# Spreading attention's reciprocal denominators over partitions: VectorE's stream shuffle in place of a 0/1 matrix product

## The chip, the cores and the metric

The kernel runs on one core of a Trainium2 chip. A core has TensorE (PE in the profile; its weight loads are listed as PEld), VectorE (DVE), ScalarE (ACT), GpSimd (POOL) and SyncE (SP), which here issues every DMA. They run side by side and wait for each other by semaphores; each one takes its own instructions in the order in which the program holds them. The metric is the device time of one execution in microseconds, the median of several runs.

## What is computed

Linear attention with an exponential feature map, followed by a gated feed-forward layer with a convolution over the sequence. Cut to what matters:

```python
batch, n_heads, seq, head_dim = (8, 8, 576, 64)      # d_feat = 128

def phi(x):
    proj = np.einsum('bhsd,df->bhsf', x, w_phi)
    proj = proj - np.max(np.abs(proj), axis=-1, keepdims=True)
    return np.concatenate([np.exp(proj), np.exp(-proj)], axis=-1)
q_p, k_p = (phi(q), phi(k))
kv = np.einsum('bhsf,bhsd->bhfd', k_p, v)
z = np.sum(k_p, axis=2)
num = np.einsum('bhsf,bhfd->bhsd', q_p, kv)
den = np.einsum('bhsf,bhf->bhs', q_p, z)[..., None] + 1e-06
attn = num / den                      # heads side by side: x of (8, 576, 512)

h = np.maximum(x @ w_in, 0.0)         # 512 -> 1024
conv_out = ...                        # 3 taps along the sequence, per column
gate = 1.0 / (1.0 + np.exp(-conv_out))
out = (h * gate) @ w_out              # 1024 -> 512
```

The place of the change is the division: `num` has a row of 576 values for each of 64 dimensions of a head, `den` has one such row per head.

## The kernel before

All matrix products are made of parts: a float32 operand is split into `hi`, its value in PE's float32r type, and `lo`, the rest, and three products (`hi·hi`, `hi·lo`, `lo·hi`) are summed in PSUM. The helper `split` (L57 to L65) does this with a copy and a subtraction on engines that the caller names.

**Layout.** Everything is transposed: features or channels lie over the 128 partitions, the sequence along the columns. A batch `b` has eight heads, in two quads `qd`; a quad has two pairs `pr`, and a pair `p = 2 qd + pr` puts two heads of 64 dimensions on the 128 partitions. The 576 positions come in five groups `g` for the attention, and in two halves `c` of 288 for the feed-forward layer (290 columns with the neighbours that the convolution needs, `HW`).

**Attention.** `k_process` loads and splits k and v, projects (`kp`, L203 to L205), takes the maximum and subtracts it on DVE (`km`, `ks`, L208 and L210), exponentiates on ACT and sums `kv` on PE (L255, L259). `q_process` does the same for q (`qp`, `qm`, `qs`), transposes on PE (`tp`, L324), exponentiates (L330), splits (`qh`, `ql`), and multiplies by `kv` (`nm`, L352 and L360). A column of ones in v makes the denominator the 65th row of `nm`. ACT copies the numerators into `num` (L383) and the denominator row into `dr` (L378), and a DMA reshapes that row into the tile `den` of 72 x 16 (L381), so that few columns have to be inverted.

**The division, `x_process` (L388 to L417).** For each batch and pair, 32 in all: DVE adds 1e-6 and inverts `den` (L396, L397); the reciprocals `rc` are split into two float32r parts (L399); four DMAs (L402) lay them out as rows 0 to 3 of the tile `rr` (two parts of two heads), a tile that exists once and is otherwise zero. Then for each half `c`: a product of `sel_r`, a 0/1 matrix made from the input `selr` at the start (L81 to L85), with 290 columns of `rr` writes into `rb` (L410): each partition gets the sum of the two parts of its head. DVE multiplies `num` by `rb` into `xf` (L412), and `xf` is split into `xh` (ACT) and `xl` (DVE), the inputs of the feed-forward layer.

**Feed-forward.** For each of 16 halves `n`: `hp` (L435, 96 products of 128x290), ReLU into `h` on ACT (L442), the convolution on POOL and DVE into `c` (L458, L463), a sigmoid (L467), a product (L471) and a split (`gh`, `gl`), and `op` (L494, 96 products of 128x288), copied out by ACT (L499) and stored (L500). The weights come in 64-bit form and are converted and split at the start (`weight_process`, L100 to L109), in large part on DVE.

**PSUM.** Three pools: `pg` with four buffers, shared by `kp`, `qp`, `tp`, `nm` and `rb`; `pm` with two, for `hp` and `op`; `pk` for the running `kv`.

**What sets the order.** A loop at the end (L564 on) runs generators as small processes, by an estimated clock `now` with PE costs (`yield pe(...)`) and delays (`yield wait(...)`), attention interleaved with feed-forward. This gives the order in which instructions are traced, with priorities: `x_process` runs under `tc.high_priority()`. A scheduler that lays the instructions on a timeline of its own then decides each engine's final order. So a change in one instruction moves others on all engines.

Of the kernel before, what the change touches and what calls it, by code (L numbers as in the profile page):

```python
# [7 lines left out]
F32 = mybir.dt.float32  # L8
F32R = mybir.dt.float32r
# [3 lines left out]
ALU = mybir.AluOpType  # L13
AX = mybir.AxisListType.X

B, H, S, D = 8, 8, 576, 64
F = 128
DM, FF = 512, 1024
P = 128
NQ = 2  # L20
TC = 288
HW = TC + 2
# [13 lines left out]
def kernel(  # L36
# [13 lines left out]
    nc = tc.nc  # L50
    cp = ctx.enter_context(tc.tile_pool(name="cp", bufs=1))
    sb = ctx.enter_context(tc.tile_pool(name="sb", bufs=1))
    pg = ctx.enter_context(tc.tile_pool(name="pg", bufs=4, space=bass.MemoryType.PSUM))
# [3 lines left out]
    def split(src, hi, lo, eng_hi, eng_lo):  # L57

        if eng_hi is nc.scalar:
            nc.scalar.activation(out=hi, in_=src, func=AF.Copy)  # L60
        elif eng_hi is nc.gpsimd:
            nc.gpsimd.tensor_scalar(out=hi, in0=src, scalar1=1.0, scalar2=0.0, op0=ALU.mult, op1=ALU.add)  # L62
        else:
            nc.vector.tensor_copy(out=hi, in_=src)
        eng_lo.tensor_tensor(out=lo, in0=src, in1=hi.bitcast(F32), op=ALU.subtract)  # L65
# [12 lines left out]
    split(wbd_f, wbd_hi, wbd_lo, nc.vector, nc.vector)  # L78
    idn = load_const(ident, [P, P], "idn")

    selr_f = sb.tile([P, P], F32, name="selr_f", tag="qr", bufs=2)  # L81
    nc.gpsimd.memset(selr_f, 0.0)
    nc.sync.dma_start(out=selr_f[:4, :], in_=selr)
    sel_r = cp.tile([P, P], F32R, name="sel_r")
    nc.gpsimd.tensor_copy(out=sel_r, in_=selr_f)  # L85
    rr = cp.tile([P, S], F32R, name="rr")
    nc.gpsimd.memset(rr.bitcast(F32), 0.0)

# [66 lines left out]
    def pe(ns):  # L157
        return ("pe", ns)
# [4 lines left out]
    def until(*keys):  # L163
        return ("until", [k for k in keys if k is not None])

    def set_ready(key, ns=0):
        ready[key] = now[0] + ns * LAT
# [136 lines left out]
    def q_process(b, qd, g):  # L304
# [80 lines left out]
        if g == 2 or g == 4:  # L385
            spawn(x_process(b, qd * 2 + g // 2 - 1))

    def x_process(b, p):  # L388
        yield ("wait", 4000)
        qd, pr = divmod(p, 2)  # L390
        dn, nt = den[b, qd, pr], numt[b, qd, pr]
        if 4 * b + p > 0:
            yield until(("x", *divmod(4 * b + p - 1, 4), 1))
        with tc.high_priority():
            rc = sb.tile([72, 16], F32, name=f"rc{b}_{p}", tag="rc", bufs=2)
            nc.vector.tensor_scalar(out=dn, in0=dn, scalar1=1e-6, scalar2=None, op0=ALU.add)  # L396
            nc.vector.reciprocal(out=rc, in_=dn)  # L397
            rhl = [sb.tile([72, 16], F32R, name=f"rc{j}{b}_{p}", tag=f"rc{j}", bufs=2) for j in range(2)]
            split(rc, rhl[0], rhl[1], nc.vector, nc.vector)  # L399
            for j in range(2):  # L400
                for i in range(2):
                    nc.sync.dma_start(out=rr[2 * j + i : 2 * j + i + 1, :].bitcast(F32).rearrange("o (r c) -> o r c", c=16),  # L402
                                      in_=rhl[j].bitcast(F32).rearrange("(r i) c -> i r c", i=2)[i])
        yield ("wait", 4500)
        for c in range(2):
            yield until(("h", 2 * (b - 1) + c) if b > 0 else None)
            t0 = 0 if c == 0 else S - HW
            with tc.high_priority():
                rb = pg.tile([P, HW], F32, name=f"rb{b}_{p}_{c}", tag="g", bufs=4)
                nc.tensor.matmul(out=rb, lhsT=sel_r, rhs=rr[:, t0 : t0 + HW], start=True, stop=True)  # L410
                xf = sb.tile([P, HW], F32, name=f"xf{b}_{p}_{c}", tag="xf", bufs=2)
                nc.vector.tensor_tensor(out=xf, in0=nt[:, t0 : t0 + HW], in1=rb, op=ALU.mult)  # L412
                xh[b, p, c] = sb.tile([P, HW], F32R, name=f"xh{b}_{p}_{c}", tag="xh", bufs=8)
                xl[b, p, c] = sb.tile([P, HW], F32R, name=f"xl{b}_{p}_{c}", tag="xl", bufs=8)
                split(xf, xh[b, p, c], xl[b, p, c], nc.scalar, nc.vector)
            set_ready(("x", b, p, c), 2500)
            yield pe(125)  # L417
# [117 lines left out]
    start = {}  # L535
# [28 lines left out]
    while moe is not None or chains or active:  # L564
        while chains and sum(1 for p in active if p[2]) < WINDOW:
            b, x, g, kind = chains.pop(0)
# [3 lines left out]
            p = active[-1]  # L570
# [10 lines left out]
        if can_a and (a_first or not can_m):  # L581
            p = active[can_a[0]]
# [66 lines left out]
```

## Time and profile before

| | |
|---|---|
| time, median of 3 runs | 837.99 us (837.19 to 838.23) |
| the profiled execution: span from first to last instruction | 955.3 us |
| its mean granted PE clock | 0.750 |
| the profiled execution's time beside the span | not recorded |

The profiled execution is longer than the runs shown, by a factor of 955.3/837.99 = 1.14. Durations below are those of the profiled execution; a time predicted for the runs has to be carried over. Two facts help in reading a busy share here: matmuls overlap their neighbours, so that a matmul's listed duration is longer than the distance from its start to the next one's, and a share over the whole span hides that the first 143 us, when weights are prepared, are not like the rest.

The groups of DMA issues name two that matter here: `rr<-rc`, 128 issues of 2.2 KB, and `den<-dr`, 96 issues of 2.0 or 0.5 KB, all from SP.

### The profile page before, as it was taken

The page shows a single profiled execution, that of the slowest core. Times are in us where ns is not written, and L with a number is a line of the kernel's source. Part 1 is how long each engine was busy: PE and PEld are TensorE (multiplying, and loading weights), DVE is VectorE, ACT ScalarE, POOL GpSimd, SP SyncE. Part 2 cuts the span into 40 slices and gives each one's busy share as a digit, 9 for nine tenths or more (in the row PEclk, how much of TensorE's full clock was granted, in tenths as well). Part 3 has the DMA queues.
Part 4 walks back from the last instruction along what each step waited for, and adds up shares of the span by engine and source line. Part 5 has one row for each costly group of instructions (what it writes and reads, how often), then busy time and mean ns, then how long its engine had stood idle before and what let it go on. Part 6 is the DMA issues. An engine that isn't in the chain of part 4 may idle for free.

```text
span 955.3 us, 18005 instructions
## 1 busy us (share of the span) xinstructions
PE 937.9 (98%) x6414; PEld 920.7 (96%) x6414; DVE 622.2 (65%) x1326; ACT 576.6 (60%) x1228; POOL 294.1 (31%) x469
## 2 busy tenths in 40 slices
PE   8999899999999999999999999999999999999998
PEld 7887799999999999999999999999999999999998
DVE  6789986887767557576665656756667575555441
ACT  4787876866667555765647556675666647533322
POOL 5668753433323213131322312313123220111010
PEclk8677777777777777777777777777777777777777
DMA  5543321112112111111211101121111100000001
GB/s 169 173 136 117 96 57 47 41 37 58 40 49 58 33 50 38 44 54 31 57 32 52 53 25 56 37 62 38 39 52 28 38 5 21 15 19 26 20 20 37
DMA packets 56336, 49.19 MB, mean 51 GB/s; under 512 B 15028, under 2 KB 54200, under 8 KB 56248
## 3 DMA queue, kind: packets, MB, share of 16 engines
q1 hardware_dynamic: 56248, 48.05, 17.5%
q8 instruction: 51, 0.84, 0.4%
q14 instruction: 37, 0.30, 0.1%
HBM read 38.14 MB, written 9.44 MB: 50 GB/s over the span
## 4 chain that ended last, share of the span: by engine, by line
PE 93%; DVE 3%; ACT 2%; issue 1%; DMA 1%; POOL 0%; SPq 0%; ACTq 0%
PE op L494 26%; PE hp L435 25%; PE kv L259 10%; PE nm L360 9%; PE tp L324 4%; PE nm L352 3%; PE kp L203 2%; PE kp L204 2%; PE kp L205 2%; PE qp L204 2%; PE qp L203 2%; PE qp L205 2%; PE kv L255 2%; PE rb L410 1%; PE qp L200 1%
## 5 line engine op out<-in xcount | busy, mean ns | idle before, releaser
L259 PEld LDWEIGHTS kv<-v,ke 128*128 128x128 f32 x1024 | 181.8, 221 | 5.2
L259 PE MATMUL kv<-v,ke 128*128 128x65 f32 x1024 | 181.8, 280 | 0.0
L463 DVE SCALAR_TENSOR_TENSOR c<-h,cw,c 128x287 f32<-128x287 f32 (+1 forms) x256 | 138.6, 550 | 59.1 <-POOL c L458 57.3
L435 PE MATMUL hp<-xl,win_hi 128*128 128x290 f32 x512 | 171.0, 334 | 0.0
L435 PE MATMUL hp<-xh,win_hi 128*128 128x290 f32 x512 | 170.9, 335 | 0.1
L494 PE MATMUL op<-gh,wout_hi 128*128 128x288 f32 x512 | 170.5, 333 | 0.0
L494 PE MATMUL op<-gh,wout_lo 128*128 128x288 f32 x512 | 170.3, 333 | 0.0
L494 PE MATMUL op<-gl,wout_hi 128*128 128x288 f32 x512 | 170.3, 333 | 0.0
L435 PE MATMUL hp<-xh,win_lo 128*128 128x290 f32 x512 | 170.1, 332 | 0.0
L458 POOL TENSOR_SCALAR c<-h,cw 128x288 f32<-128x288 f32 x128 | 73.0, 571 | 264.1 <-ACT h L442 234.6
L62 POOL TENSOR_SCALAR kxh<-kr 128x256 fp32r<-128x256 f32 (+1 forms) x80 | 38.6, 482 | 259.0 <-PE kp L204 252.6
L65 DVE TENSOR_TENSOR ql<-qe,qh 128x512 fp32r<-128x512 f32 x112 | 77.6, 707 | 45.7 <-ACT qh L60 45.6
L435 PEld LDWEIGHTS hp<-xh,win_hi 128*128 128x128 f32 x512 | 104.4, 205 | 1.0 <-ACT os L499 0.6
L435 PEld LDWEIGHTS hp<-xh,win_lo 128*128 128x128 f32 x512 | 104.2, 204 | 0.2
L435 PEld LDWEIGHTS hp<-xl,win_hi 128*128 128x128 f32 x512 | 103.6, 202 | 0.2
L494 PEld LDWEIGHTS op<-gh,wout_hi 128*128 128x128 f32 x512 | 103.7, 203 | 0.0
L494 PEld LDWEIGHTS op<-gh,wout_lo 128*128 128x128 f32 x512 | 103.5, 202 | 0.1
L442 ACT ACTIVATE h<-hp 128x290 f32<-128x290 f32 x128 | 52.4, 411 | 84.4 <-PE hp L435 83.9
L494 PEld LDWEIGHTS op<-gl,wout_hi 128*128 128x128 f32 x512 | 103.2, 202 | 0.1
L378 ACT ACTIVATE dr<-nm 1x512 f32<-1x512 f32 (+1 forms) x96 | 46.3, 483 | 77.7 <-PE nm L360 48.6
L208 DVE TENSOR_REDUCE km<-kp 128x4 f32<-128x512 f32 (+1 forms) x80 | 50.6, 633 | 59.5 <-PE kp L205 59.1
L330 ACT ACTIVATE qe<-tp 128x512 f32<-128x512 f32 x112 | 61.7, 597 | 39.0 <-PE tp L324 37.3
(88 smaller groups left out, 2125.1 us busy)
## 6 DMA issues: line engine op xcount, KB each, us to landing
v<-in_vt_dram SPq DMA_DIRECT2D x80, 130.0 KB
out_dram<-os SPq DMA_DIRECT2D x64, 144.0 KB
qr<-in_qT_dram SPq DMA_DIRECT2D x64, 128.0 KB
kr<-in_kT_dram SPq DMA_DIRECT2D x64, 128.0 KB
w_r<-in_w_in_dram SPq DMA_DIRECT2D x8, 512.0 KB
w_r<-in_w_out_dram SPq DMA_DIRECT2D x8, 512.0 KB
rr<-rc SPq DMA_DIRECT2D x128, 2.2 KB
qr<-in_qT_dram SPq DMA_DIRECT2D x16, 64.0 KB
```

Of the source, the lines that this page charges most:

```text
L62: nc.gpsimd.tensor_scalar(out=hi, in0=src, scalar1=1.0, scalar2=0.0, op0=ALU.mult, op1=ALU.add)
L65: eng_lo.tensor_tensor(out=lo, in0=src, in1=hi.bitcast(F32), op=ALU.subtract)
L208: nc.vector.tensor_reduce(out=m, in_=ps3, axis=AX, op=ALU.max, apply_absolute_value=True)
L259: ins = nc.tensor.matmul(out=kp[i][:, s, p0 : p0 + VW], lhsT=lhsT, rhs=v[:, (2 * t + i) * VW : (2 * t + i + 1) * VW], start=False, stop=(g ...
L330: nc.scalar.activation(out=e, in_=tp.rearrange("p i t s -> p i (t s)"), func=AF.Exp, scale=1.0 - 2.0 * s)
L360: ins = after(ins, lambda: nc.tensor.matmul(out=ps[:, i, o : o + w], lhsT=w_, rhs=x_, start=(k == 0), stop=(k == 5)))
L378: nc.scalar.activation(out=dro.rearrange("o (r i c) -> o i r c", i=2, c=16), in_=ps[D : D + 1, :, o : o + w].rearrange("o i (r c) -> o i r ...
L435: nc.tensor.matmul(out=ps, lhsT=w_, rhs=x_, start=(k == 0), stop=(k == 11))
L442: nc.scalar.activation(out=hs, in_=ps, func=AF.Relu)
L458: nc.gpsimd.tensor_scalar(out=cv, in0=hs[:, o : o + TC], scalar1=cw[:, f, 1:2], scalar2=0.0, op0=ALU.mult, op1=ALU.add)
L463: nc.vector.scalar_tensor_tensor(out=cv[:, lo:hi], in0=hs[:, o + j - 1 + lo : o + j - 1 + hi], scalar=cw[:, f, j : j + 1], in1=cv[:, lo:hi ...
L494: nc.tensor.matmul(out=ps, lhsT=w_, rhs=x_, start=(k == 0), stop=(k == 23))
```

## The change

The product with the 0/1 matrix is taken out, with the matrix, its load and the split of the reciprocals. `rr` becomes a float32 tile, and the four DMAs of a pair now write the same unsplit reciprocals into rows 0, 32, 64 and 96: the first head's into 0 and 32, the second head's into 64 and 96. For each half, DVE's stream shuffle, with a mask of 32 zeros, copies within each group of 32 partitions the first partition's row to all 32, from `rr` into `xf`; the multiply then takes `num` and `xf` and writes `xf` in place. The number of DMAs stays, and so does the generators' code around them (`yield pe(125)` included).

```diff
-    selr_f = sb.tile([P, P], F32, name="selr_f", tag="qr", bufs=2)
-    nc.gpsimd.memset(selr_f, 0.0)
-    nc.sync.dma_start(out=selr_f[:4, :], in_=selr)
-    sel_r = cp.tile([P, P], F32R, name="sel_r")
-    nc.gpsimd.tensor_copy(out=sel_r, in_=selr_f)
-    rr = cp.tile([P, S], F32R, name="rr")
-    nc.gpsimd.memset(rr.bitcast(F32), 0.0)
+    rr = cp.tile([P, S], F32, name="rr")
+    nc.gpsimd.memset(rr, 0.0)
...
             nc.vector.reciprocal(out=rc, in_=dn)
-            rhl = [sb.tile([72, 16], F32R, name=f"rc{j}{b}_{p}", tag=f"rc{j}", bufs=2) for j in range(2)]
-            split(rc, rhl[0], rhl[1], nc.vector, nc.vector)
-            for j in range(2):
-                for i in range(2):
-                    nc.sync.dma_start(out=rr[2 * j + i : 2 * j + i + 1, :].bitcast(F32).rearrange("o (r c) -> o r c", c=16),
-                                      in_=rhl[j].bitcast(F32).rearrange("(r i) c -> i r c", i=2)[i])
+            for i in range(2):
+                for j in range(2):
+                    row = D * i + 32 * j
+                    nc.sync.dma_start(out=rr[row : row + 1, :].rearrange("o (r c) -> o r c", c=16),
+                                      in_=rc.rearrange("(r i) c -> i r c", i=2)[i])
...
             with tc.high_priority():
-                rb = pg.tile([P, HW], F32, name=f"rb{b}_{p}_{c}", tag="g", bufs=4)
-                nc.tensor.matmul(out=rb, lhsT=sel_r, rhs=rr[:, t0 : t0 + HW], start=True, stop=True)
                 xf = sb.tile([P, HW], F32, name=f"xf{b}_{p}_{c}", tag="xf", bufs=2)
-                nc.vector.tensor_tensor(out=xf, in0=nt[:, t0 : t0 + HW], in1=rb, op=ALU.mult)
+                nc.vector.stream_shuffle(out=xf, in_=rr[:, t0 : t0 + HW], mask=[0] * 32)
+                nc.vector.tensor_tensor(out=xf, in0=nt[:, t0 : t0 + HW], in1=xf, op=ALU.mult)
```

Where the order moves. In the rows below a tile's name is followed by indices (the batch is left out, then pair or quad, and half or group) and a running number; line numbers after the change are 4 to 6 lower.

First place: DVE at the first pair of the first batch. Before, the reciprocal is followed by its split, and the multiplies that use it come 31 rows behind the split:

```order
L396 TENSOR_SCALAR den_0_0_505<-den_0_0_505 72x16
L397 RECIPROCAL rc_0_834<-den_0_0_505 72x16
L64 CAST rc_0_837<-rc_0_834 72x16
L65 TENSOR_TENSOR rc_0_838<-rc_0_834,rc_0_837 72x16
L102 TENSOR_SCALAR w_t<-w_r 128x512
L104 SCALAR_TENSOR_TENSOR w_t<-w_r,w_t 128x512
L208 TENSOR_REDUCE km_0_0_716<-kp_0_0_712 128x2
```

After it, from the same reciprocal:

```order
L393 RECIPROCAL rc_0_829<-den_0_0_500 72x16
L98 TENSOR_SCALAR w_t<-w_r 128x512
L100 SCALAR_TENSOR_TENSOR w_t<-w_r,w_t 128x512
L204 TENSOR_REDUCE km_0_0_711<-kp_0_0_707 128x2
L103 SCALAR_TENSOR_TENSOR w_t<-w_t,w_r 128x512
L204 TENSOR_REDUCE qm_1_1_721<-qp_1_1_718 128x4
L206 TENSOR_TENSOR ks_0_0_713<-kp_0_0_707,km_0_0_711 128x256
L96 TENSOR_SCALAR w_t<-w_r 128x512
L206 TENSOR_TENSOR qs_1_1_723<-qp_1_1_718,qm_1_1_721 128x512
L204 TENSOR_REDUCE qm_1_2_736<-qp_1_2_733 128x4
L405 STREAM_SHUFFLE xf_0_0_948<-rr 128x290
L405 STREAM_SHUFFLE xf_0_1_955<-rr 128x290
```

The two shuffles, which need the four DMAs into `rr`, stand nine rows behind the reciprocal.

Second place: PE at the same pair. Before, two `rb` products stand between a transposition and a projection of k:

```order
L324 MATMUL tp_1_3_949<-idn,qs_1_3_832 128x128 x4
L410 MATMUL rb_0_0_957<-rr,sel_r 128x290
L410 MATMUL rb_0_1_965<-rr,sel_r 128x290
L203 MATMUL kp_0_3_973<-wbd_hi,kxh_0_3_847 128x256
L204 MATMUL kp_0_3_973<-wbd_lo,kxh_0_3_847 128x256
```

After it the projection follows the transposition:

```order
L320 MATMUL tp_1_3_940<-idn,qs_1_3_827 128x128 x4
L199 MATMUL kp_0_3_962<-wbd_hi,kxh_0_3_838 128x256
L200 MATMUL kp_0_3_962<-wbd_lo,kxh_0_3_838 128x256
L201 MATMUL kp_0_3_962<-wbd_hi,kxl_0_3_839 128x256
L199 MATMUL kp_0_3_962<-wbd_hi,kxh_0_3_838 128x256
```

Both `rb` are gone; the rows around them are otherwise alike.

Third place: DVE in the middle, at the last pair (3) of the third batch. Before, its multiplies are followed by the gate's work, and the next pair's multiply comes 28 rows later:

```order
L412 TENSOR_TENSOR xf_3_0_4384<-num_1_1_3434,rb_3_0_4382 128x290
L65 TENSOR_TENSOR ql_1_1_4790<-qe_1_1_0_4791,qh_1_1_4789 128x512
L412 TENSOR_TENSOR xf_3_1_4392<-num_1_1_3434,rb_3_1_4390 128x290
L65 TENSOR_TENSOR ql_1_1_4790<-qe_1_1_1_4795,qh_1_1_4789 128x512
L65 TENSOR_TENSOR xl_3_0_4387<-xf_3_0_4384,xh_3_0_4386 128x290
L463 SCALAR_TENSOR_TENSOR c_3744<-h_7_3627,cw,c_3744 128x288
L65 TENSOR_TENSOR xl_3_1_4395<-xf_3_1_4392,xh_3_1_4394 128x290
```

After it:

```order
L405 STREAM_SHUFFLE xf_3_0_4307<-rr 128x290
L457 SCALAR_TENSOR_TENSOR c_3685<-h_6_3554,cw,c_3685 128x287
L405 STREAM_SHUFFLE xf_3_1_4314<-rr 128x290
L457 SCALAR_TENSOR_TENSOR c_3685<-h_7_3569,cw,c_3685 128x288
L406 TENSOR_TENSOR xf_3_0_4307<-num_1_1_3377,xf_3_0_4307 128x290
L406 TENSOR_TENSOR xf_3_1_4314<-num_1_1_3377,xf_3_1_4314 128x290
L457 SCALAR_TENSOR_TENSOR c_3685<-h_7_3569,cw,c_3685 128x287
L65 TENSOR_TENSOR xl_3_0_4311<-xf_3_0_4307,xh_3_0_4310 128x290
L65 TENSOR_TENSOR xl_3_1_4318<-xf_3_1_4314,xh_3_1_4317 128x290
L405 STREAM_SHUFFLE xf_0_0_4906<-rr 128x290
L405 STREAM_SHUFFLE xf_0_1_5051<-rr 128x290
L465 TENSOR_TENSOR c_3685<-c_3685,h_0_3183 128x288
```

The shuffles of the next batch's first pair now stand seven rows behind the last pair's second shuffle, ahead of the gate's work (L465).

## Prediction

> **What bounds the kernel now.** I read the page first, for the busy shares, the granted clock and the chain that ended last.
>
> ```profile
> span 955.3 us, 18005 instructions
> PE 937.9 (98%) x6414; PEld 920.7 (96%) x6414; DVE 622.2 (65%) x1326; ACT 576.6 (60%) x1228; POOL 294.1 (31%) x469
> PEclk8677777777777777777777777777777777777777
> PE 93%; DVE 3%; ACT 2%; issue 1%; DMA 1%; POOL 0%; SPq 0%; ACTq 0%
> ```
>
> TensorE (PE) is busy 98% of the span and carries 93% of the chain; VectorE (DVE) is at 65%. Since an average hides stages, the view of windows comes next, cut into the start, the stage in which the weights are still being prepared and the first MoE block runs, the long middle, and the end.
>
> ```profile
> core 0: us, PE busy (x) PEld busy (x) DVE busy (x) ACT busy (x) POOL busy (x), PEclk, DMA share, GB/s
> 0.00:72.00 72.00, 65.75 (x374) 56.79 (x374) 51.96 (x97) 49.37 (x103) 43.67 (x57) 0.75 0.54 159
> 72.00:143.00 71.00, 63.28 (x424) 58.35 (x422) 64.93 (x120) 53.82 (x117) 49.63 (x58) 0.73 0.32 91
> 143.00:812.00 669.00, 668.94 (x4750) 666.65 (x4749) 441.14 (x960) 423.68 (x905) 184.38 (x324) 0.75 0.15 42
> 812.00:860.00 48.00, 48.00 (x302) 47.70 (x301) 26.46 (x65) 21.27 (x45) 7.44 (x14) 0.75 0.06 17
> ```
>
> From 143 to 860 us PE has no gap at all (668.94 of 669, then 48 of 48) at a constant clock of 0.75. There, time is PE work and nothing else. Only from 72 to 143 is another engine level with it: DVE is busy 64.93 of 71 us there, PE 63.28. So the change has to be weighed twice, once as PE work taken out of a full PE, once as DVE work and DVE waits in a stage where DVE is nearly full.
>
> **What is removed from PE.** Each of the 64 `rb` products (L410, 128x290) goes. The duration of a matmul in a group is no price, since matmuls overlap; the pitch is. The chain, merged, gives it:
>
> ```profile
> 833.66 0.34 PE rb L410 x2
> 843.90 15.54 PE hp L435 x96
> ```
>
> 96 products of the same 128x290 shape take 15.54 us, 162 ns each; two `rb` take 0.34 us. 64 x 0.162 = **10.4 us** of PE. In the middle and at the end nothing covers that, so it comes off the span in full, unless something else becomes late.
>
> By the Trainium skill, "TensorE: Matmul & The Clock Gate", section "Back-to-back issue gap", a warm product of 290 columns would take 290/2.4 + 2.5 = 123 ns, an estimate by which the term would be 7.9 us. The trace says 162 ns at a granted clock of 0.75, and that same page's two-state clock (half or full) isn't what these rows show; the measured pitch stands.
>
> **Waits around `rb`.** By the windows PE's gaps lie in the first 143 us and at the very end. Of its waits these five are at `rb` or at the `kp` product that can follow it:
>
> ```profile
> PE rb L410 <- ACT qh L330: 1.5, 1, 1.5
> PE kp L203 <- DVE xf L412: 1.4, 1, 1.4
> PE kp L203 <- issue: 1.1, 2, 0.8
> PE rb L410 <- DVE ks L210: 1.1, 1, 1.1
> PE rb L410 <- ACT num L383: 1.0, 1, 1.0
> PE qp L200 <- DMA qr<-in_qT_dram: 4.1, 1, 4.1
> ```
>
> The first five sum to 6.1 us (the sixth is the wait for the first data, with which the program begins): `rb` takes one of the four PSUM buffers of the pool that `kp`, `qp`, `tp` and `nm` share, and waits for one or makes the next tile wait. Such a gap also costs clock:
>
> ```profile
> 87.00:90.00 3.00, 1.66 (x8) 1.41 (x8) 3.00 (x7) 2.66 (x7) 3.00 (x4) 0.64 0.31 71
> 90.00:93.00 3.00, 3.00 (x16) 2.80 (x16) 3.00 (x9) 2.83 (x6) 2.50 (x4) 0.57 0.46 162
> ```
>
> At 0.64 and 0.57 in place of 0.75 these 6 us do (0.11 + 0.18)/0.75 x 3 = 1.2 us less work. If all of it goes, the gain is up to 6.1 + 1.2 = 7.3 us on top. The buffers that come free are asked for by the next tile at once, though, and DVE, which drains them, is full there. So I keep 0 to 7.3 as bounds.
>
> **What DVE gains and loses.** Removed are the split of the reciprocals (64 small instructions); added are 64 shuffles of 128x290 float32; the multiply stays but reads two SBUF tiles.
>
> ```profile
> L65 DVE TENSOR_TENSOR rc<-rc,rc 72x16 fp32r<-72x16 f32 x32 | 7.0, 220 | 0.3
> L64 DVE CAST rc<-rc 72x16 fp32r<-72x16 f32 x32 | 6.9, 217 | 0.4
> L64 DVE CAST kvh<-kvf 128x260 fp32r<-128x260 f32 x28 | 9.2, 329 | 11.6 <-ACT kvf L283 11.3
> L65 DVE TENSOR_TENSOR ql<-qe,qh 128x512 fp32r<-128x512 f32 x112 | 77.6, 707 | 45.7 <-ACT qh L60 45.6
> L65 DVE TENSOR_TENSOR xl<-xf,xh 128x290 fp32r<-128x290 f32 x64 | 31.1, 494 | 5.5 <-ACT xh L60 5.2
> L412 DVE TENSOR_TENSOR xf<-num,rb x64: 431/449/459, 72.4 to 860.5; 128x290 f32<-128x290 f32 x64
> L65 DVE TENSOR_TENSOR xl<-xf,xh x64: 443/454/996, 74.9 to 862.1; 128x290 fp32r<-128x290 f32 x64
> ```
>
> 7.0 + 6.9 = 13.9 us go. No shuffle is in the trace. Its bounds are the one-input cast of 260 columns (329 ns) and the 512-column subtraction (707 ns); I take 0.45 us, the multiply of its own shape. 64 x 0.45 = 28.8 us (21 to 45). The Trainium skill, "VectorE: DVE Perf Modes", section "The perf-mode tier table", gives the shuffle about 2400 ns at 2048 columns and one column a cycle: scaled to 290 an estimate of 0.57 us, 36 us in all, which no run here shows.
>
> Of the last two rows (shortest, median and longest), the one with a PSUM input never leaves 431 to 459 ns, the one with two SBUF inputs reaches 996. The new multiply is of the second kind; if it is stretched like `xl` (mean 494 ns against the median of 449 here), that is 64 x 0.045 = 2.9 us more. The Trainium skill, "SBUF — State Buffer", section "SBUF: two separate sides", says why: such an instruction and one of GpSimd lock each other out of a shared port. The 996 ns agree with it.
>
> Net, DVE goes from 622 to about 622 - 13.9 + 28.8 + 2.9 = 640 us, with bounds 629 to 656: at most 69% of the span. In the middle that is hidden under PE. Between 72 and 143 us lie the first 8 multiplies: 8 x 0.45 = 3.6 us are added, and 4 splits go, of which the one below took 0.70 + 0.15 us: 3.4 us at that rate. In that stage the two cancel. I cost DVE's work at 0.
>
> ```profile
> 89.30 0.70 DVE L64 CAST rc<-rc 72x16 fp32r<-72x16 f32 x1
> 91.22 0.15 DVE L65 TENSOR_TENSOR rc<-rc,rc 72x16 fp32r<-72x16 f32 x1
> ```
>
> **The wait that is moved.** `rr` is filled by four DMAs. Before, PE's `rb` would wait for them, late in its queue; now DVE's shuffle does, and behind it stand the maxima, the subtractions and the weight conversions that PE and ScalarE need. How long does `rr` take?
>
> ```profile
> 87.52 0.24 DVE L397 RECIPROCAL rc<-den 72x16 f32<-72x16 f32 x1
> 90.06 1.61 SPq L402 DMA_DIRECT2D rr<-rc  x2
> 94.38 0.72 SPq L402 DMA_DIRECT2D rr<-rc  x1
> 50.03 0.54 SPq L381 DMA_DIRECT2D den<-dr  x1
> 51.80 0.17 DVE L396 TENSOR_SCALAR den<-den 72x16 f32<-72x16 f32 x1 [1.29 <-DMA den<-dr]
> L402 SPq DMA_DIRECT2D rr<-rc x128: 709/736/1711, 52.5 to 828.8; - x128
> ```
>
> A like DMA landed 51.80 - 50.57 = 1.2 us after its issue ended. At 87.52 the last `rr` issue ended at 95.10, so `rr` was there 8.8 us after the reciprocal began, with two loads between and the split ahead. At best, without either, it is 0.24 + 4 x 0.74 + 1.2 = 4.4 us. The order of the changed kernel puts nine rows between reciprocal and shuffle in the first place (some 9 x 0.54 + 0.24 = 5.1 us, by 64.93 us for 120 instructions). So a shuffle there waits 0 to 3.7 us. Five pairs stand that close in the first 200 rows (9, 10, 9, 13 and 11 rows between); the bound is 0 to 18 us. I take 0.5 us each, near the best case, since the split that delayed the issue is gone: 2.5 us, against some 3 of the waits around `rb` that go. **Net of the early stage: 0**, bounds -7.3 to +18.
>
> In the middle the order has shuffles of one pair seven rows behind the last ones of the pair before. Since `rr` is a single tile, its DMAs must wait for those; seven rows at 0.45 to 0.55 us are 3.5 us, against 4 x 0.74 + 1.2 = 4.2: DVE stands about 1 us there. That it is hidden is shown by waits of the same kind:
>
> ```profile
> DVE den L396 <- DMA den<-dr: 28.3, 19, 3.6
> DVE xf L412 <- PE rb L410: 12.3, 11, 2.6
> ```
>
> DVE waited for a DMA up to 3.6 us at a time while PE lost nothing. The second row goes altogether. SP still issues four DMAs a pair, its queue holds `kr`, `qr`, `v` and output issues behind them as before. POOL loses a memset and a copy at the start, where PE waits 4.1 us for its first data.
>
> **Sum.** 955.3 - 10.4 + 0 = **944.9 us** of profiled span, 0.9891 of it. The profile gives no time beside the span, and the runs shown have a median of 837.99 us, 0.877 of it: they ran faster than the profiled execution. If that is the clock alone, it was 0.75/0.877 = 0.855 there, and the gain scales alike: 10.4 x 0.877 = 9.1 us. At a clock of 1.0 the products would take 10.4 x 0.75 = 7.8 us. Forecast **828.9 us**; its own range 822 (all 7.3 us gained too: 937.6 x 0.877) to 835.5 (only 7.8 gained, and 6 x 0.877 = 5.3 lost early).
>
> **Rivals.**
> 1. *The shuffle's wait stalls DVE where it is full.* Decides if more than 10.4/5 = 2.1 us for each of the five early pairs reaches PE. At 2 us the gain is eaten (838); at 3 us, 15 us lost, span 959.9, **842 us**, slower. For it: 64.93 of 71 us busy. Against: DVE's 6.1 idle us in that stage absorb part, and `rr` is issued sooner than before.
> 2. *The timed runs aren't PE-bound throughout.* At full clock PE's 937.9 us would be 703, and 838 would hold waits on others; taking out PE work then gives little, and DVE's 18 us cost something. Time 834 to 840, say **837**. For it: 838 against 955. Against: in the trace PE leaves no gap for 717 us, so even some speed-up leaves it first.
> 3. *More than the products goes*, the early waits and clock dips too, with a new order that is better: **822 us**.
>
> **How the numbers follow.** Forecast 0.66; rival 1 0.16 (half near 838, half slower); rival 2 0.13 (0.05 faster, 0.05 the same, 0.03 slower); rival 3 0.05. A difference below 0.2% (1.7 us) can't be told from none here. Faster 0.66 + 0.05 + 0.05 = 0.76; same 0.08 + 0.05 = 0.13; slower 0.08 + 0.03 = 0.11. For 8 in 10 the range takes the forecast's and reaches into rivals 1 and 2: 822 to 838.
>
> **What would show it.** Right: no `rb`; PE still without gaps from about 143 us, at the same clock; the stretch from there to the end shorter by some 9 us; DVE's busy time near 640 us and the shuffle near 0.45 us. Wrong: PE idle between 48 and 143 us above 12 us with `kp` or `hp` waiting for DVE, and DVE's shuffle waiting for the `rr` DMA by 2 us and more; or gaps of PE in the middle, behind a late `ks`, `qs` or `xl`. A different granted clock would make the two spans incomparable, then the timed runs alone decide.

## The result, and the profile after

| | before | after |
|---|---|---|
| time, median of 4 runs each | 837.59 us (836.79 to 838.23) | 825.10 us (824.99 to 825.60) |
| ratio, 95% interval | | 0.9854 [0.984, 0.9868] |
| profiled execution: span, mean granted PE clock | 955.3 us, 0.750 (the one of the prediction); 836.6 us, 0.984 (a later one) | 823.5 us, 0.989 |

The change takes 12.5 us off, 1.5%. The prediction said 828.9, 9.1 us off, with a range of 822 to 838. The time lies in the range, and the gain is 3.4 us larger than forecast.

The profiled execution of before from which the prediction was made had a granted clock of 0.75 and the one of after has 0.989, so these two can't be laid side by side; a later execution of the unchanged kernel (run e5_before) had 0.984, and it takes the place of before below.

The page of after, its span, busy times, granted clock and chain:

```profile
span 823.5 us, 17817 instructions
PE 788.0 (96%) x6350; PEld 772.5 (94%) x6350; DVE 645.6 (78%) x1390; ACT 569.5 (69%) x1228; POOL 307.6 (37%) x467
PEclk9799989999999999999999999999999999999999
PE 74%; DVE 10%; ACT 7%; issue 4%; DMA 3%; POOL 1%; SPq 1%; DVEq 0%; ACTq 0%; POOLq 0%
```

The page of before, in the later execution:

```profile
span 836.6 us, 18005 instructions
PE 801.4 (96%) x6414; PEld 784.9 (94%) x6414; DVE 627.0 (75%) x1326; ACT 573.4 (69%) x1228; POOL 306.6 (37%) x469
```

PE has 64 instructions fewer and is busy 13.4 us less; DVE has 64 more and is busy 18.6 us more. PE's busy time is a rough measure here: three executions of the changed kernel's order (after, e8_after, e12_after_w) have 788.0, 789.9 and 791.5 us of it in spans of 823.5 to 823.6 us. PE's idle time as a whole didn't shrink: 836.6 - 801.4 = 35.2 us before, 823.5 - 788.0 = 35.5 after. It lies elsewhere, and DVE's time went up by more than the whole gain while the kernel became faster; both have to be looked at by stage. The windows of before, in the later execution:

```profile
core 0: us, PE busy (x) PEld busy (x) DVE busy (x) ACT busy (x) POOL busy (x), PEclk, DMA share, GB/s
72.00:143.00 71.00, 58.90 (x426) 54.41 (x427) 65.69 (x121) 53.25 (x115) 48.92 (x56) 0.90 0.31 89
200.00:700.00 500.00, 495.82 (x4150) 492.99 (x4149) 379.53 (x830) 359.06 (x774) 170.66 (x284) 1.00 0.18 50
```

And of after:

```profile
72.00:143.00 71.00, 56.99 (x439) 52.01 (x439) 68.79 (x128) 54.54 (x120) 48.03 (x58) 0.95 0.33 96
200.00:700.00 500.00, 499.65 (x4190) 497.52 (x4189) 403.33 (x888) 368.10 (x797) 173.13 (x284) 1.00 0.18 50
```

Early, DVE is now busy 68.79 of 71 us and PE has 14 us of gaps in that stretch, 2 more than before. In the middle it is the other way round: PE's gaps of 4.2 us in 500 have shrunk to 0.35. At a clock near 1.0 the middle of *before* isn't gapless, as it was at 0.75.

Where along the program did the 13.1 us between these two profiles come off? ScalarE's sigmoid of each feed-forward half (n = 0 to 15) is a good milestone. Its starts, from the timelines of ScalarE (the last two columns belong to experiments below):

| start of the sigmoid of half n, us | before | after (e8_after) | before, other delay (e11) | after, other delay (e12) |
|---|---|---|---|---|
| n = 1 | 200.20 | 199.96 | 198.04 | 200.41 |
| n = 3 | 308.57 | 303.91 | 304.97 | 303.94 |
| n = 11 | 699.29 | 688.22 | 694.10 | 688.35 |
| n = 15 | 810.00 | 796.87 | 805.46 | 797.00 |

By n = 1 after is 0.2 us ahead, by n = 3 4.7, by n = 11 11.1, by n = 15 13.1. A milestone doesn't say how far PE has come with everything else, though; its counts do. These are the windows of the tile `op` up to n = 1 and from there to n = 15, of before and then of e8_after (PE's busy time and count, then those of its weight loads and of ScalarE):

```profile
0.00:200.20 200.20, 5.27 (x39) 5.28 (x40) 0.41 (x1) 0.93 0.35 103
200.20:810.00 609.80, 194.68 (x1326) 181.51 (x1326) 22.12 (x55) 1.00 0.16 45
```

```profile
0.00:199.96 199.96, 8.31 (x63) 8.43 (x63) 0.82 (x2) 0.95 0.35 104
199.96:796.87 596.91, 188.28 (x1302) 177.63 (x1302) 21.64 (x54) 1.00 0.16 46
```

At n = 1 PE's other groups have equal counts, but for 14 of the 64 `rb` that before has behind it; at n = 15 all counts but `rb` are equal. With 133 ns a product (worked out below), the 24 products of `op` that after is ahead at n = 1 are 3.2 us. So the early stage is not level: after leads by 0.2 + 3.2 = 3.4 us there, of which its 14 missing products make 1.9 and 1.5 is something else (three executions of after's order differ by up to 0.45 us at n = 1). From there to n = 15 it gains 12.9 - 3.2 = 9.7 us, against 6.7 for the other 50 products and 3.8 for the gaps of the middle, 10.5 in all. Most of the gain is made from 200 us on, and products and gaps account for it to within 1 us.

The groups of the tile `xf` in after (shortest, median and longest duration in ns, first and last start, shapes), then the new operations among DVE's groups by form (busy us, mean ns, idle time before):

```profile
L405 DVE LOAD_MASK_SELECT xf<-rr x64: 3/8/17, 59.7 to 743.6; - x64
L405 DVE STREAM_SHUFFLE xf<-rr x64: 472/483/506, 59.7 to 743.6; 128x290 f32<-128x290 f32 x64
L406 DVE TENSOR_TENSOR xf<-num,xf x64: 442/450/1184, 62.6 to 744.8; 128x290 f32<-128x290 f32 x64
L65 DVE TENSOR_TENSOR xl<-xf,xh x64: 435/453/1546, 65.9 to 746.3; 128x290 fp32r<-128x290 f32 x64
```

```profile
L406 DVE TENSOR_TENSOR xf<-num,xf 128x290 f32<-128x290 f32 x64 | 32.0, 522 | 0.0
L405 DVE STREAM_SHUFFLE xf<-rr 128x290 f32<-128x290 f32 x64 | 29.0, 484 | 0.4 <-issue 0.4
```

The same places in before, in the later execution:

```profile
L412 DVE TENSOR_TENSOR xf<-num,rb 128x290 f32<-128x290 f32 x64 | 27.9, 445 | 1.3 <-PE rb L410 1.2
L65 DVE TENSOR_TENSOR rc<-rc,rc 72x16 fp32r<-72x16 f32 x32 | 7.8, 243 | 0.3
L64 DVE CAST rc<-rc 72x16 fp32r<-72x16 f32 x32 | 7.0, 219 | 0.4
```

A shuffle takes 483 ns with almost no scatter, and the multiply's mean went from 445 to 522 ns while its median stayed at 450: a few are stretched to as much as 1184 ns.

### The profile page after: what moved, and what is told of

It is laid out like the page before. It is cut to its first block, busy times and chain, and to the rows that moved or that the text cites. A ratio compares the mean times of both kernels' runs of the same rounds, so it can differ in the third digit from the quotient of the medians.

```text
span 823.5 us, 17817 instructions
## 1 busy us (share of the span) xinstructions
PE 788.0 (96%) x6350; PEld 772.5 (94%) x6350; DVE 645.6 (78%) x1390; ACT 569.5 (69%) x1228; POOL 307.6 (37%) x467
## 4 chain that ended last, share of the span: by engine, by line
PE 74%; DVE 10%; ACT 7%; issue 4%; DMA 3%; POOL 1%; SPq 1%; DVEq 0%; ACTq 0%; POOLq 0%
PE op L488 22%; PE hp L429 21%; PE kv L255 8%; PE nm L356 8%; PE tp L320 3%; PE kp L199 2%; PE nm L348 2%; PE kp L200 2%; PE kp L201 2%; PE qp L199 1%; PE qp L200 1%; PE qp L201 1%; DMA w_r<-in_w_in_dram 1%; PE kv L251 1%; DVE qm L204 1%
## 5 line engine op out<-in xcount | busy, mean ns | idle before, releaser
L255 PE MATMUL kv<-v,ke 128*128 128x65 f32 x1024 | 159.4, 255 | 1.4 <-ACT ke L236 1.2
L255 PEld LDWEIGHTS kv<-v,ke 128*128 128x128 f32 x1024 | 153.5, 193 | 4.8 <-ACT ke L236 1.8
L429 PE MATMUL hp<-xh,win_hi 128*128 128x290 f32 x512 | 153.2, 300 | 0.6 <-ACT os L493 0.6
L429 PE MATMUL hp<-xl,win_hi 128*128 128x290 f32 x512 | 152.7, 298 | 0.2 <-DVE xl L65 0.2
L488 PE MATMUL op<-gh,wout_hi 128*128 128x288 f32 x512 | 152.2, 298 | 0.0
L429 PE MATMUL hp<-xh,win_lo 128*128 128x290 f32 x512 | 151.9, 297 | 0.0
L488 PE MATMUL op<-gl,wout_hi 128*128 128x288 f32 x512 | 151.4, 296 | 0.0
L488 PE MATMUL op<-gh,wout_lo 128*128 128x288 f32 x512 | 150.9, 295 | 0.0
L236 ACT ACTIVATE ke<-ks 128x512 f32<-128x512 f32 (+1 forms) x80 | 46.9, 586 | 39.1 <-DVE ks L206 36.5
L326 ACT ACTIVATE qe<-tp 128x512 f32<-128x512 f32 x112 | 61.2, 595 | 12.2 <-PE tp L320 10.4
L356 PE MATMUL nm<-ql,kvh 128*65 128x256 f32 x224 | 68.4, 308 | 0.3 <-DVE ql L65 0.2
```

The costliest lines, as they stand in the source:

```text
L236: nc.scalar.activation(out=e[:, 0], in_=pr, func=AF.Exp)
L255: ins = nc.tensor.matmul(out=kp[i][:, s, p0 : p0 + VW], lhsT=lhsT, rhs=v[:, (2 * t + i) * VW : (2 * t + i + 1) * VW], start=False, stop=(g ...
L326: nc.scalar.activation(out=e, in_=tp.rearrange("p i t s -> p i (t s)"), func=AF.Exp, scale=1.0 - 2.0 * s)
L356: ins = after(ins, lambda: nc.tensor.matmul(out=ps[:, i, o : o + w], lhsT=w_, rhs=x_, start=(k == 0), stop=(k == 5)))
L429: nc.tensor.matmul(out=ps, lhsT=w_, rhs=x_, start=(k == 0), stop=(k == 11))
L488: nc.tensor.matmul(out=ps, lhsT=w_, rhs=x_, start=(k == 0), stop=(k == 23))
```

## The experiments

Theory: the time is PE's work in the middle, and the 64 products are 8 to 9 us of it. Rivals for the rest of the gain: the waits at the product's PSUM buffer and its turn in PE's queue; DVE's load; and a luckier order of everything else, since any edit makes the scheduler lay all engines out anew. A letter in an expectation stands for the theory that it states.

**The kernels repeated.** The unchanged kernel, twice, and the changed one.

> The kernel before, unchanged, for a profile at a granted clock near that of the changed kernel's profile (0.989; before's own was taken at 0.750). Theory A (PE work plus the early waits around rb): time 837.6 us, within 0.2% of before; PE without gaps from about 160 us; PE's pitch 133 ns for 128x288 as after; the first 143 us hold about 4 us more PE idle than after's. Theory B (the new order is what gained): PE's idle time differs from after's in the middle as well, by some us. Theory C (the runs are not PE-bound): PE idle of 50 us and more.

> The kernel before once more, for a profile at a granted clock near 0.99. Theory D (of the 12.5 us, 8.4 are PE work, some 8 are the product's PSUM buffer and place, and DVE's extra work costs some 4): PE's idle time is some 4 us and more above that of the changed kernel's profile (35.5 us), and part of it lies behind 160 us. Theory A (PE work, and early waits alone, DVE free): the same 4 us, all of it before 143 us, none in the middle.

> The changed kernel unchanged, on the same chip as the others of this call, so that they can be compared with it: 0.984 to 0.987 of before, 825 us, PE idle near 35 us at a clock of 0.99.

e1_before: 837.29 us, ratio to its copy 0.9987 [0.9972, 1.0002]. e5_before: 838.43 us, a single run. e8_after: 826.0 us, 0.9866 [0.9845, 0.9887]. The result repeats within 1 us on other occasions, and differences of 2 us are real here. e1_before's profiled execution had a granted clock of 0.558 and decides nothing between the theories; e5_before's does. Theories A and D both expected some 4 us more idle time of PE than after has, and missed: 35.2 against 35.5 us. What theory B said is seen, idle time that differs in the middle (4.2 against 0.35 us of 500), and in the first 143 us it differs the other way.

**The work of the products alone.** After, with 64 products of 128x290 put back on PE where no buffer and no other engine is involved: the first of each group of `hp`, overwritten by the real one.

```diff
+            if f < 4:
+                nc.tensor.matmul(out=ps, lhsT=win_hi[0][:, f * P : (f + 1) * P], rhs=xh[b, 0, c], start=True, stop=True)
```

> The changed kernel with 64 extra products of 128x290 on PE, four for each half at the start of an hp tile, whose results are overwritten: PE work comes back, without its PSUM buffer and without its waits. Theory A: 64 x 0.134 = 8.6 us more than after, 833.0 to 834.5 us. Theory C (not PE-bound): under 3 us more, 825 to 828 us. A result above 836 would say that the place of the work matters beyond its pitch.

833.48 us, 0.995 [0.9924, 0.9975]: 7.5 us more than e8_after and 8.4 more than the first result, as theory A had it. PE's middle is nearly full in it too (498.75 of 500 us). The order of the other engines changed with this edit as well, so its time need not be the products' work alone. The chain of e8_after gives a like price per product:

```profile
716.10 12.80 PE op L488 x96
730.72 11.49 PE hp L429 x84
742.21 12.80 PE op L488 x96
```

12.80 / 96 = 133 ns for a product of `op` (288 columns). Between the two runs of `op` lie the 96 products of an `hp` (290 columns; the chain's row holds the last 84): 742.21 - 728.90 = 13.31 us, 139 ns each, the steps from one PSUM tile to the next included. 64 products are 8.5 to 8.9 us by this. So some 4 us of the 12.5 are something else.

**The product with its buffer.** After, with a product into a buffer of `pg` as before, and the multiply reading it; the shuffle stays and its result isn't used. It is a product with another weight matrix on `rr` (a float32r tile again), so the output differs from the reference's.

```diff
+                rb = pg.tile([P, HW], F32, name=f"rb{b}_{p}_{c}", tag="g", bufs=4)
+                nc.tensor.matmul(out=rb, lhsT=wbd_hi[:, :P], rhs=rr[:, t0 : t0 + HW], start=True, stop=True)
...
-                nc.vector.tensor_tensor(out=xf, in0=nt[:, t0 : t0 + HW], in1=xf, op=ALU.mult)
+                nc.vector.tensor_tensor(out=xf, in0=nt[:, t0 : t0 + HW], in1=rb, op=ALU.mult)
```

> The changed kernel with the product into rb back in its place and its PSUM buffer, read by the multiply; the shuffle stays but its result is overwritten (the output is then not the reference's: the product uses other weights). Theory A: product (8.6 us) and buffer waits (4 us) come back: 836.5 to 839 us. Theory B (order, or the split that is gone): the product alone comes back: 832 to 835 us.

841.86 us, 1.0052 [1.0026, 1.0079]: above every range expected. A second version lets the product read a weight tile in place of `rr`, so that PE never waits for the reciprocals (`rhs=win_hi[0][:, :HW]`).

> As e3_buf (product into rb with its PSUM buffer, read by the multiply, shuffle kept but its result overwritten, so the output is not the reference's), but the product reads a weight tile in place of rr, so that PE has nothing to wait for but the buffer. e3_buf took 841.9 us where the same PE work without buffer and place (e2_work) took 833.5. If the 8.4 us between them are the PSUM buffer: 839 to 843 us here. If they are PE's in-order wait for rr behind the DMAs: 832 to 836 us.

845.08 us, 1.0086 [1.0068, 1.0104]. So it isn't PE's wait for `rr`. The same 64 products cost 7.5 us in e2_work, 16 in e3_buf and 19 in e9_bufconst (each against e8_after). Part of the extra are gaps of PE in the middle, as the window of e3_buf shows (4.6 us idle of 500):

```profile
200.00:700.00 500.00, 495.40 (x4152) 492.25 (x4151) 389.40 (x869) 364.60 (x781) 170.96 (x285) 1.00 0.18 50
```

At this point a price for the buffer and its turn in the queue looked likely. PE's list of waits for this stretch doesn't bear it out: none is at `rb`, in e3_buf or in e9_bufconst, and the largest is at a tile of another PSUM pool (of e3_buf):

```profile
PE op L490 <- ACT os L495: 2.3, 2, 1.1
```

**DVE's load.** More of it: after, with every shuffle done twice (one line added). Less of it: before, without the split of the reciprocals (four DMAs lay out the unsplit ones, and two rows of the 0/1 matrix count).

> The changed kernel with each shuffle made twice: 64 x 0.484 = 31 us more on DVE. Theory A (DVE is hidden under PE but for the early stage): 0 to 4 us more (8 shuffles of the first batch at 0.484 us), 825 to 829 us. Rival (at 78% busy DVE is near the bound and its work shows): 8 us and more, above 833 us.

> The kernel before without the split of the reciprocals (the unsplit ones go to rows 0 and 1 of rr, rows 2 and 3 get weight 0 in the 0/1 matrix): product and PSUM buffer as before, 64 small DVE instructions (14 us) less. Theory D (DVE work shows at about 0.4 us for 1): 837.6 - 5.6 = 832 us, between 829 and 834. Theory A (DVE is hidden): 836 to 838 us.

e4_shuf2: 838.72 us, 1.0001 [0.9983, 1.0018], 13 us slower for 19 us of DVE, the rival's side. e6_noboth: 832.68 us, 0.9942 [0.9925, 0.9959], 4.8 faster than its copy of before for 11 us of DVE less (615.9 against 627.0). Both seem to say that DVE's time costs. If so, versions of after with less of it must win. Two were tried: the multiply on GpSimd (`nc.gpsimd.tensor_tensor`), and one shuffle of 576 columns into a tile `xw` and one multiply in place for each pair:

```diff
+            nc.vector.stream_shuffle(out=xw, in_=rr, mask=[0] * 32)
+            nc.vector.tensor_tensor(out=nt, in0=nt, in1=xw, op=ALU.mult)
...
-                nc.vector.stream_shuffle(out=xf, in_=rr[:, t0 : t0 + HW], mask=[0] * 32)
-                nc.vector.tensor_tensor(out=xf, in0=nt[:, t0 : t0 + HW], in1=xf, op=ALU.mult)
+                xf = nt[:, t0 : t0 + HW]
```

> The changed kernel with the multiply by the shuffled reciprocals on GpSimd in place of DVE: 32 us less on DVE (78% busy), some 50 more on POOL (37% busy). Theory D: 32 x 0.4 = 13 us less than the changed kernel, 811 to 818 us, if GpSimd's longer multiply does not make xl late. Theory A: 823 to 826 us.

> The changed kernel with one shuffle and one multiply over all 576 columns of a pair, in place in num, instead of two of each over 290: DVE loses 64 instructions and by the durations of like rows (0.48 and 0.50 us for 290 columns, 0.3 us for 286 columns more) about 15 us. Theory D (DVE work shows at 0.3 to 0.4): 5 us less than the changed kernel, 819 to 822 us, faster than both. Rival (the earlier single shuffle, five to nine rows behind the reciprocal, makes DVE wait for rr and gives it back): 825 us or more.

Both missed. e7_pool: 847.16 us, 1.0119 [1.0095, 1.0144]. Its page:

```profile
PE 797.6 (94%) x6350; PEld 781.4 (93%) x6350; DVE 646.2 (77%) x1326; ACT 574.0 (68%) x1228; POOL 362.1 (43%) x531
```

Its multiply among the groups of `xf` (shortest, median, longest), and DVE's costliest group:

```profile
L406 POOL TENSOR_TENSOR xf<-num,xf x64: 687/816/1548, 59.7 to 765.3; 128x290 f32<-128x290 f32 x64
```

```profile
L457 DVE SCALAR_TENSOR_TENSOR c<-h,cw,c 128x288 f32<-128x288 f32 (+1 forms) x256 | 147.8, 587 | 45.0 <-POOL c L452 42.2
```

DVE has 64 instructions fewer and is busy as long as in after (645.6): what GpSimd took over, 32 us, came back as longer instructions on DVE (9 us of it in the convolution, whose mean went from 554 to 587 ns). e10_full: 836.74 us, 0.9989 [0.9974, 1.0003]. Its groups of `xf`, and its middle in the view of windows:

```profile
L402 DVE STREAM_SHUFFLE xf<-rr x32: 784/810/828, 59.6 to 729.2; 128x576 f32<-128x576 f32 x32
L403 DVE TENSOR_TENSOR num<-num,xf x32: 741/750/1225, 62.5 to 730.3; 128x576 f32<-128x576 f32 x32
```

```profile
200.00:700.00 500.00, 494.20 (x4135) 490.89 (x4135) 399.16 (x808) 362.71 (x779) 186.25 (x284) 1.00 0.18 50
```

A shuffle of 576 columns takes 810 ns against 2 x 483, so the operations themselves became cheaper, and no product came back. DVE as a whole is nevertheless busy 650.2 us, 4.6 more than in after, and PE has 5.8 us of gaps in the middle. A price of 0.3 to 0.4 for each us of DVE would make under 2 us of those 4.6, where the run lost 11; in e7_pool DVE's time is unchanged and 21 us are lost. So the theory that prices DVE's microseconds falls, and neither kernel has the product's buffer. What all of these share is another order on every engine.

**The order alone.** Both kernels with one estimated delay of the planner changed, in `x_process`. The work stays the same. In before the order changes: up to 161 us PE's matmuls stand in the trace of e11_before_w as in that of e5_before, and from the 959th of 6,414 on they differ. In after it doesn't: the delay changes the order in which the kernel is traced, and with it running numbers in the tiles' names, but the scheduler arrives at the same program, and in the trace of e12_after_w the instructions of every engine stand in the order of after's trace from the first to the last.

```diff
-        yield ("wait", 4500)
+        yield ("wait", 5500)
```

> The kernel before with the planner's delay in x_process raised from 4500 to 5500, and nothing else: the same instructions and the same result in another order. It measures how much the order alone moves the time. Theory O (the 4 us that the change gained beyond its products are a luckier order): this run differs from the kernel before by 3 us or more in either direction (below 834.5 or above 840.5), with PE's busy time between 200 and 700 us moved from 495.8. Theory G (they belong to the product's buffer and its turn in PE's queue): within 1.5 us of the kernel before (836 to 839), gaps of 3 to 5 us in that stretch as before.

> The kernel after with the same delay raised from 4500 to 5500, and nothing else. Theory O: it loses its lead in part, 828 us or more, with PE busy less than 498 of the 500 us between 200 and 700. Theory G: 824 to 827 us, with PE busy 499 us or more of the 500, whatever the order; the lead over the same-delay kernel of before stays 11 to 13 us.

e11_before_w: 834.24 us (833.33 to 835.25), 0.9955 [0.9938, 0.9971], 3.8 us faster than before, by order alone. e12_after_w: 825.76 us (825.51 to 826.11), 0.9852 [0.9825, 0.9878], the same as after. By e11_before_w theory O holds for the kernel before: another order alone is worth 3.8 us there. e12_after_w lies where theory G put it, but decides nothing: the edit left the order as it was, so this run repeats after, and no other order of the unchanged work of after was measured. The lead over the better of the two orders of before isn't 11 to 13 us but 834.24 - 825.76 = 8.5. The middle of e11_before_w and then of e12_after_w:

```profile
200.00:700.00 500.00, 497.62 (x4180) 495.40 (x4179) 385.50 (x835) 363.06 (x783) 176.36 (x284) 1.00 0.18 50
```

```profile
200.00:700.00 500.00, 499.66 (x4190) 497.54 (x4188) 403.87 (x888) 367.89 (x797) 173.05 (x284) 1.00 0.18 50
```

The gaps of before went from 4.2 to 2.4 us in this stretch; those of after stay at 0.34, as they must in an unchanged order. By the milestones the other order of before saves 3.6 us by n = 3 and 4.5 by n = 15, and 0.4 of this was there before the first matmul that differs. What remains between e11 and e12 from n = 3 to n = 11, four batches with 32 products, is 389.13 - 384.41 = 4.7 us; the products alone are 32 x 0.133 = 4.3.

No version was found that beats after.

## Why the prediction was right, and where its sizes were off

**The products (10.4 us of profiled span, 9.1 of a run): right in kind, a little too large.** Their pitch at full clock is 133 ns by `op` and 139 by `hp`, on which the 162 was read, not 0.877 x 162 = 142, and 64 of them are 8.5 to 8.9 us. e2_work gives 7.5 to 8.4 back, and the better order of before lies 8.5 above after. By the Trainium skill, "TensorE: Matmul & The Clock Gate", section "Back-to-back issue gap", the estimate was 123 ns and 7.9 us; at full clock it is 10 ns below the pitch of `op` where the scaled pitch is 9 ns above it, and its 7.9 us lie inside what e2_work gave back.

**The early stage (net 0): nearly so as a sum, by other waits than those it was made of.** Beside its products after is 1.5 us ahead at n = 1, though the windows of 72 to 143 us show DVE fuller by 3.1 us and PE idle for 1.9 us more. Of the two waits that were set against each other, the one at `rb` did go, but others took its place. The three largest rows of PE's waits between 48 and 143 us in before, then in after:

```profile
PE rb L410 <- ACT num L383: 3.2, 2, 1.7
PE rb L410 <- ACT qh L330: 2.2, 1, 2.2
PE kp L203 <- DVE xf L412: 1.9, 1, 1.9
```

```profile
PE tp L320 <- DVE ks L206: 4.0, 3, 3.4
PE qp L196 <- ACT qh L326: 2.5, 2, 1.5
PE kp L199 <- POOL wout_lo L65: 2.0, 1, 2.0
```

All rows of these lists sum to 16.1 us before and 17.8 after. That they come out nearly alike is in part luck: the forecast had some 3 us of waits at `rb` against 2.5 at the shuffle, and neither size nor the second wait is what came. (PE's 12 idle us between 48 and 143, which were to be a sign of being wrong, are exceeded at full clock by both kernels and tell nothing.) No shuffle before 143 us waited for a DMA, so rival 1 doesn't occur. All its waits lie later. DVE's row for 143 to 824 us (us in total, times, longest):

```profile
DVE xf L405 <- DMA rr<-rc: 15.6, 7, 3.7
```

**The shuffle's stand in the middle, "about 1 us", hidden: hidden, but larger.** It was 2.2 us a time (15.6 / 7) and up to 3.7. PE's whole list of waits in the same stretch says what it cost:

```profile
PE qp L199 <- issue: 0.8, 1, 0.8
PE hp L429 <- ACT os L493: 0.6, 3, 0.2
PE nm L356 <- ACT qh L60: 0.6, 2, 0.4
PE nm L356 <- DVE ql L65: 0.2, 1, 0.2
```

PE waits for DVE once, for 0.2 us.

**DVE's net, 622 to 640 us, in a sum of +18: measured +18.6 (627.0 to 645.6).** Its parts came out near the forecast too: 29.0 us for the shuffles where 28.8 was forecast; 4.1 us more for the multiply (32.0 against 27.9) where 2.9 was; 14.8 us removed where 13.9 was. The Trainium skill, "VectorE: DVE Perf Modes", section "The perf-mode tier table", gave an estimate of 0.57 us for the shuffle: the trace has 0.483, as in the nearest rows. Its page "SBUF — State Buffer", section "SBUF: two separate sides", says that a DVE instruction with two SBUF inputs and one of GpSimd that reads SBUF shut each other out: the multiply's longest went from 459 ns (in the profile of the prediction) to 1184 when its second input moved from PSUM to SBUF, and e7_pool's stretched DVE groups agree with it.

**The step that was mis-sized: "time there is PE work and nothing else", from 143 us on.** It was read from an execution at a clock of 0.75, in which PE's slowness gave every other engine slack. The waiting stretches of before at full clock, between 200 and 700 us (PE's list of waits in the later execution):

```profile
PE nm L360 <- ACT qh L330: 1.1, 1, 1.1
PE rb L410 <- DVE ks L210: 1.0, 1, 1.0
PE tp L324 <- DVE xf L412: 0.8, 1, 0.8
PE qp L203 <- issue: 0.7, 3, 0.2
PE hp L435 <- ACT h L442: 0.6, 2, 0.3
```

They are many places and no single cause; in after and e8_after this list is empty. The gain was underrated by 3.4 us and the products overrated by 0.2 to 0.6, which makes about 4 us beyond the products' work; 3.8 of them are the gaps of the middle that went. e11_before_w gains 3.8 with the products still in: another order of before does without much of that loss as well (1.8 us of it in the middle). So rival 3, "waits go too, with a new order that is better", joined the forecast, for the most part in the middle and not early where it was put. That the total still fell inside the range, which reached down to 822 for early waits, owes something to luck. The conversion was the second slip: 0.877 was read as a clock of 0.855 in the runs. In the later execution the clock was 0.984, and 35.2 us of its span are idle time of PE. Rival 2 had that premise right in kind (though PE's work shrank to 801.4 us there and not to 703), and its consequence wrong: the kernel isn't bound by PE throughout, and about the work of 64 products still came off.

**What stays open.** Why PE has next to no gaps in the middle in the order of after, and more of them in before, e3_buf, e4_shuf2, e7_pool and e10_full, wasn't settled. Each of the edits, e2_work and e6_noboth included, changes the work and the order at once, and two orders of before and one of after are a small sample: whether the change itself leads to the better order, or happened on it, is not shown. That the product's buffer or DVE's load has a price of its own in the middle is neither shown nor excluded; that PE never waits at `rb` in the middle of e3_buf speaks against a price of the buffer.

## What to carry to other kernels

Where PE is nearly gapless, price what is taken off it by pitch (the length of a run of like matmuls by their number), and expect that much; here some 8.5 us came off although DVE took 18.6 us on. Where a scheduler lays out all engines anew, an edit brings a second, unplanned change with it: move one neutral number of the planner in both kernels, see in the traces that the order did move in both (here it moved in one), and compare, before a microsecond beyond the work is given a cause. A milestone such as one engine's sigmoid compares two kernels only where the counts of the other work are equal. And look at the granted clock before a stage is called bound by PE, since a slow PE hides the gaps that a full clock shows.

## What the runs showed of the hardware that was not expected

- The granted clock differs between executions of one program: the unchanged kernel was profiled at 0.750, 0.558 (span 1251.3 us) and 0.984, with the same value through most of the span each time. These are means by slice and don't show what the clock does within one.
- From a clock of 0.75 to 1.0 the pitch of a float32r product of 288 columns (`op`) went from 15.34 / 96 = 160 to 133 ns, a factor of 1.20, and that of 290 columns (`hp`) from 162 to 139, 1.16, where the clock's factor is 1.33: a part of it doesn't follow the clock. The row of before for `op`:

```profile
859.44 15.34 PE op L494 x96
```

- VectorE's stream shuffle of float32 takes 483 ns for 290 columns and 810 for 576, which is 1.14 ns a column and some 150 ns beside it; its mask costs an instruction of 8 ns each time.
- GpSimd's multiply of 128x290 float32 has a median of 816 ns against 450 on VectorE, and moving 64 of them there left VectorE's busy time where it was.
